# Block-sorted attention and a maxout MLP on one Trainium2 core: the hand-written order of the first batch item's steps is replaced by another

## The chip, the cores and the metric

The kernel runs on one core of a Trainium2 chip. The metric is the device time of one execution in microseconds, as the median of several runs. Lower is better. All times below are microseconds unless marked otherwise.

The engines are named as the profile names them: PE is TensorE's matmuls and PEld its weight loads, DVE is VectorE, ACT is ScalarE, POOL is GpSimd, SP is SyncE. POOL and SP mostly issue DMAs here.

## The reference

There are 4 batch items of 8 heads, 768 tokens and a head dimension of 64. Each head's tokens are cut into 8 blocks of 96. A small matrix per head is normalized five times by rows and columns, and mixes the key and value blocks. Each query block then attends to its own mixed block, and the result goes through an MLP with a maxout.

```python
P = sort_net                                  # (4, 8, 8, 8)
for _ in range(5):
    P = np.exp(P - np.max(P, axis=-1, keepdims=True))
    P = P / (np.sum(P, axis=-1, keepdims=True) + 1e-09)
    P = P / (np.sum(P, axis=-2, keepdims=True) + 1e-09)
k_sorted = np.einsum('bhij,bhjcd->bhicd', P, k_b)
v_sorted = np.einsum('bhij,bhjcd->bhicd', P, v_b)
scores = scale * np.matmul(q_b, k_sb.transpose(0, 1, 2, 4, 3))
attn = softmax(scores)                        # over the 96 keys of the block
x = np.matmul(attn, v_sb)                     # to (3072, 512)
...
out = np.maximum(x @ w1, x @ w2) @ w_out      # w1, w2: (512, 1024); w_out: (1024, 512)
```

## The kernel before

The kernel computes the maxout as `relu(x @ (w1 - w2)) @ w_out + x @ (w2 @ w_out)`. So `w1` is first replaced by the difference (`w_difference`, four quarters of the columns), and the product of `w2` and `w_out` is computed once (`w2_transposes`, then `w_product`).

The work of one item is cut into steps. Each step is a run of matmuls into one PSUM tile, followed by one eviction (or two instructions for the values) on VectorE or ScalarE. The steps that the change reorders are these, with the names that the order's text gives them:

- `k0` to `k2` (`sort_k`, line 449): mix a third of the keys' block positions with the sort matrix, 32 matmuls, eviction into `kT`.
- `v0` to `v3` (`sort_v`, line 473): the same for a quarter of the value dimensions, 16 matmuls, eviction into `v_sb`. Every one of them needs the whole of `v_dc`, which `turn_v` (line 242) makes from the raw values.
- `tq0`, `tq1` (`q_transposes`, line 413): transposes of two head pairs of the queries, 24 matmuls, eviction into `qT`.
- `SC0` to `SC7` (`scores`, line 539): 8 matmuls, then an exp on ScalarE into an `e` buffer. Scores 0, 1, 4, 5 read the first half of `qT`, and 2, 3, 6, 7 the second.
- `VA0` to `VA7` (`values`, line 567): 8 matmuls with `e` of the same number as weights, then a reciprocal (`rs`) and a product (`x`) on VectorE. It needs all of `v_sb`.
- `tx0` to `tx3` (`x_transposes`, line 600): transposes of two values' results, eviction into `xT`.
- `tw0`, `tw1` (`w2_transposes`, line 634): transposes of half of `w2`, eviction into `w2T`.
- `hcta`, `hctb` (`moe_h_products` and `moe_h`, lines 670 and 685): the two halves of the products of one hidden pair of tiles, 4 matmuls each. `c` is the half of the tokens, `t` the quarter of the hidden columns. The `a` half needs `tx0` (`c`=0) or `tx2` (`c`=1), the `b` half `tx1` or `tx3`. The relu eviction follows the `b` half.
- `diff2`, `diff3`: `w_difference` on VectorE. Differences 0 and 1 are done by POOL, ahead of this order.
- `pe2` (`block_diagonals`, line 312): the sort matrices for the later items, 5 matmuls and seven VectorE instructions.

A letter `A` or `D` at the end of a name fixes the eviction's engine, ScalarE or VectorE. `F` and a digit adds a 512-column matmul of zeros (`keep_streaming`, line 77) ahead of the matmuls of the next scores, values or first h half. The first key step has 640 such columns.

All engines take their own instructions in the order of the program (`manual_schedule`). All PSUM tiles come from one pool of four buffers (`psum`, tag `ps`), so a step's matmuls also wait until an earlier step's eviction has left a buffer. A pair of h halves holds its buffer from the `a` half to the eviction.

The order of the first item's steps is the text `front`. Between its last 26 steps and the ones before them, the POOL queue is given the loads of the next items' queries, values and keys. After `front`, the loops over the items run, with steps of the next item woven between products of the present one by the tables `first_tail`, `second_tail` and `third_tail`. They begin with the second item's keys (`KS`).

Of the kernel before, what the change touches and what calls it, by code (L numbers as in the profile page):

```python
# [16 lines left out]
def kernel(  # L17
# [752 lines left out]
    for b in range(1, B):  # L770
# [10 lines left out]
    turn_v(first, "D", 80, 96)  # L781

    front = """
        k0D k1A k2D v1D v2A v3A tq0D v0A tq1D SC1 SC0 F1
        SC2 VA1 SC5 VA0 SC3 F2 VA2 SC4 F0 tx0D SC6 VA3
        SC7 h00a VA4 tx1A tw0D h01a VA5 h01bA diff2 h00bA VA7 tx2A
        tw1A h02a VA6 h02bA h11a diff3 tx3A h12a h03a h12bD h10a h10bA
        pe2 h11bD h03bA h13a h13bA
    """.split()
    fills = [0]  # L790

# [170 lines left out]
```

The softmax here doesn't subtract the row's maximum and nothing guards it: scores larger than these inputs give would overflow.

## Time and profile before

| | |
|---|---|
| median of 4 runs | 166.57 us (166.44 to 167.0) |
| the profiled execution's own time | 166.44 us |
| its span | 164.7 us |
| PE busy | 159.1 us, 97% of the span |
| DVE busy | 76.3 us, 46% |
| ACT busy | 83.1 us, 50% |
| first key sort of item 0 starts | 11.94 us |
| first key sort of item 1 starts | 38.24 us |

The span runs from the first to the last instruction of the program on the core. The device time has 1.7 us more around it. Busy time of PE is an upper view, since its matmuls overlap. Times in the timeline and in the chain of waits count from the start of the span. The stretch between the two last rows of the table is the first item's front, in which the changed order stands.

### The profile page before, as it was taken

The numbers are of one execution on the slowest core, as the hardware profiler recorded it, in microseconds if no ns is written. First come the engines' busy times: TensorE is split into PE (matmuls) and PEld (weight loads), VectorE is DVE, ScalarE is ACT, GpSimd is POOL, SyncE is SP. The second block draws the span as 40 slices with busy tenths as digits, with TensorE's granted clock in tenths as the row PEclk, the third lists the DMA queues.
The fourth block names the chain that finished last, engine by engine and source line by source line (L and its number), as shares of the span: only waits on it lengthen the run. The fifth ranks groups of instructions, "written<-read, shape, count | busy, mean of one in ns | idle before, by whom it ended". The sixth has DMA issues, their size and how long they took to land.

```text
span 164.7 us, 4563 instructions
## 1 busy us (share of the span) xinstructions
PE 159.1 (97%) x2018; PEld 96.3 (58%) x2018; DVE 76.3 (46%) x169; ACT 83.1 (50%) x102; POOL 32.6 (20%) x59
## 2 busy tenths in 40 slices
PE   7999799999999999999999999999999999999992
PEld 7958578756554555557655554575655546654451
DVE  4879678556375564535277863250642320000011
ACT  3586895918239846055652262557447206642020
POOL 7999397140104000000014010000000000000000
DMA  3999999999999996688425999691025294000333
GB/s 48 204 205 197 199 208 205 210 203 221 212 202 211 219 236 100 175 116 218 90 27 100 192 189 234 166 226 23 0 52 175 50 164 142 0 0 0 127 131 127
DMA packets 30404, 23.90 MB, mean 145 GB/s; under 512 B 16752, under 2 KB 25200, under 8 KB 30384
## 3 DMA queue, kind: packets, MB, share of 16 engines
q0 software_dynamic: 11040, 13.37, 48.2%
q1 hardware_dynamic: 19200, 10.17, 26.9%
q8 instruction: 16, 0.26, 0.6%
q10 hardware_dynamic: 144, 0.07, 0.1%
q14 instruction: 4, 0.03, 0.1%
HBM read 26.75 MB, written 6.29 MB: 201 GB/s over the span
## 4 chain that ended last, share of the span: by engine, by line
PE 89%; DVE 5%; ACT 2%; issue 1%; DMA 1%
PE out_ps L704 38%; PE h_ps L677 26%; PE o_ps L575 5%; PE wc_ps L657 4%; PE k_ps L458 4%; PE s_ps L548 4%; PE tq_ps L433 2%; PE v_ps L479 1%; PE v_ps L523 1%; PE tw_ps L638 1%; ACT e L556 1%; DMA p_sb<-in_sort_net_dram 1%; PE tx_ps L613 1%; DVE colsum L276 1%; DVE p_sb L273 1%
## 5 line engine op out<-in xcount | busy, mean ns | idle before, releaser
L704 PE MATMUL out_ps<-wo_sb,g 128*128 128x512 bf16 (+2 forms) x200 | 48.3, 371 | 0.1
L677 PE MATMUL h_ps<-xT,w_sb 128*128 128x384 bf16 x256 | 44.5, 326 | 0.0
L677 PEld LDWEIGHTS <-w_sb 128*128 128x128 bf16 x256 | 24.0, 98 | 15.6
L556 ACT ACTIVATE e<-s_ps 96x768 bf16<-96x768 f32 x32 | 23.9, 804 | 13.9 <-PE s_ps L548 13.7
L691 ACT ACTIVATE g<-h_ps 128x768 bf16<-128x768 f32 x27 | 21.8, 811 | 17.4 <-PE h_ps L677 17.3
L704 PEld LDWEIGHTS <-g 128*128 128x128 bf16 x200 | 17.1, 97 | 15.8
L704 PE MATMUL out_ps<-wc,xT 128*128 128x512 bf16 (+2 forms) x100 | 24.8, 370 | 0.0
L108 ACT COPY o<-out_ps 128x1024 f32<-128x1024 f32 x10 | 10.1, 1012 | 28.0 <-PE out_ps L704 25.2
L592 DVE TENSOR_TENSOR x<-o_ps,rs 96x512 bf16<-96x512 f32 x32 | 22.0, 687 | 1.1
L704 PEld LDWEIGHTS <-xT 128*128 128x128 bf16 x100 | 9.6, 97 | 11.2
L575 PEld LDWEIGHTS <-e 96*128 96x128 bf16 x256 | 11.8, 97 | 5.9 <-DVE v_sb L110 0.2
L586 DVE RECIPROCAL rs<-o_ps 96x8 f32<-96x8 f32 x32 | 6.4, 201 | 18.0 <-PE o_ps L575 17.8
L739 DVE COPY o<-out_ps 128x512 f32<-128x512 f32 (+1 forms) x2 | 1.2, 624 | 27.6 <-PE out_ps L704 27.6
L575 PE MATMUL o_ps<-v_sb,e 96*128 96x65 bf16 x256 | 12.9, 193 | 0.0
L110 DVE CAST kT<-k_ps 128x1024 bf16<-128x1024 f32 x7 | 8.3, 1216 | 9.2 <-PE k_ps L458 9.2
L108 ACT CAST v_sb<-v_ps 96x1024 bf16<-96x1024 f32 x10 | 9.8, 1013 | 2.4 <-PE v_ps L479 0.9
L693 DVE TENSOR_SCALAR g<-h_ps 128x768 bf16<-128x768 f32 x5 | 4.8, 957 | 10.8 <-PE h_ps L677 10.8
L110 DVE CAST v_sb<-v_ps 96x1024 bf16<-96x1024 f32 x6 | 7.3, 1218 | 5.1 <-PE v_ps L523 2.2
L548 PE MATMUL s_ps<-qT,kT 64*128 64x96 bf16 x256 | 8.6, 204 | 1.0 <-PE o_ps L575 0.8
L160 POOL DMA_DIRECT2D v_raw<-in_k_dram x3 | 2.5, 833 | 35.2 <-DVE v_dc L250 31.4
L548 PEld LDWEIGHTS <-kT 64*128 64x128 bf16 x256 | 6.1, 94 | 5.8 <-issue 4.0
L169 POOL DMA_DIRECT2D v_raw<-in_v_dram x11 | 5.9, 540 | 13.7 <-DVE v_dc L250 8.3
(95 smaller groups left out, 144.5 us busy)
## 6 DMA issues: line engine op xcount, KB each, us to landing
out_dram<-o SPq DMA_DIRECT2D x11, 512.0 KB, 3.2
v_raw<-in_v_dram POOLq DMA_DIRECT2D x8, 384.0 KB, 12.5
k_raw<-in_k_dram POOLq DMA_DIRECT2D x9, 256.0 KB, 10.0
w_sb<-in_moe_w_dram POOLq DMA_DIRECT2D x4, 256.0 KB, 9.8
w_sb<-in_moe_w_dram POOLq DMA_DIRECT2D x2, 512.0 KB, 11.2
wo_sb<-in_moe_w_out_dram POOLq DMA_DIRECT2D x2, 512.0 KB, 14.6
v_raw<-in_v_dram POOLq DMA_DIRECT2D x3, 256.0 KB, 4.8
q_raw<-in_q_dram POOLq DMA_DIRECT2D x4, 192.0 KB, 9.0
```

The costliest lines, as they stand in the source:

```text
L108: nc.scalar.copy(out=out_ap, in_=in_ap)
L110: nc.vector.tensor_copy(out=out_ap, in_=in_ap)
L458: nc.tensor.matmul(ps[r0 : r0 + 64, m * 64 : (m + 1) * 64], kv[r0 : r0 + 64, t * 16 + m, :], bd_k[b][r0 : r0 + 64, :], start=True, stop=True,)
L548: nc.tensor.matmul(ps[:, h2 * 512 + ii * 128 : h2 * 512 + ii * 128 + BLK], kT[b][rows, (hp * 8 + i) * BLK : (hp * 8 + i) * BLK + 128], rhs ...
L556: nc.scalar.activation(out=e[:, 0 : 8 * BLK].rearrange("p (t c r) -> p t c r", t=8, r=R), in_=ps[0:BLK] .rearrange("p (t f) -> p t f", t=8 ...
L575: nc.tensor.matmul(ps[:, h2 * 512 + ii * 65 : h2 * 512 + (ii + 1) * 65], e[:, (h2 * 4 + ii) * BLK : (h2 * 4 + ii) * BLK + 128], v_sb[:, m0 ...
L586: nc.vector.reciprocal(out=rs, in_=ov[:, :, :, 64])
L592: nc.vector.tensor_tensor(out=x, in0=ov[:, :, :, 0:D], in1=rs.to_broadcast([BLK, 2, 4, D]), op=ALU.mult,)
L657: nc.tensor.matmul(ps[:, 0:512], w2T[:, fb, dmt * 128 : (dmt + 1) * 128], wo_sb[:, fb, :], start=(fb == 0), stop=(fb == NFB - 1),)
L677: nc.tensor.matmul(h_ps[ch, t][:, m * 512 : m * 512 + TCH], w1_sb[:, hp, fb * 128 : (fb + 1) * 128], xT[:, b % 2, ch, hp % 2, hp // 2, :], ...
L691: nc.scalar.activation(out=g, in_=src, func=AF.Relu)
L704: nc.tensor.matmul(dst, g_tiles[b, ch, m // 2][:, m % 2, off : off + 128] if m < NFB else xT[:, b % 2, ch, hp % 2, hp // 2, off : off + 12 ...
```

## The change

The text `front` is replaced. The same steps are in it, with these differences:

- The first key tile leaves PSUM by ScalarE, not VectorE. The value tiles come in the order 0, 3, 1, 2 with the first on VectorE, where they came as 1, 2, 3, 0.
- After the first two scores come one values step and one scores step, where it was scores first. There are four fills, not three.
- `SC6` and `SC5` stand next to each other; `SC7` comes only after `VA5`. `tw0` and `tx1` stand ahead of the first h products.
- `diff3` stands ahead of `VA5` and `diff2` after it.
- Seven steps follow `pe2`, where four did.
- Transposes 2 and 3 of x are evicted by VectorE instead of ScalarE, and of the eight h tiles VectorE takes three (`h03`, `h13`, `h10`), where it took two.

No function is changed.

```diff
     front = """
-        k0D k1A k2D v1D v2A v3A tq0D v0A tq1D SC1 SC0 F1
-        SC2 VA1 SC5 VA0 SC3 F2 VA2 SC4 F0 tx0D SC6 VA3
-        SC7 h00a VA4 tx1A tw0D h01a VA5 h01bA diff2 h00bA VA7 tx2A
-        tw1A h02a VA6 h02bA h11a diff3 tx3A h12a h03a h12bD h10a h10bA
-        pe2 h11bD h03bA h13a h13bA
+        k0A k1A k2D v0D v3A v1A tq0D v2A tq1D SC1 SC0 F3
+        VA1 SC3 F0 VA0 SC2 F2 VA3 SC4 F1 tx0D VA2 SC6
+        SC5 tw0D tx1A h00a h01a VA6 h00bA VA4 diff3 h01bA VA5 SC7
+        diff2 tw1A h03a VA7 h03bD h02a tx2D h02bA tx3D h13a pe2 h10a
+        h13bD h10bD h12a h11a h12bA h11bA
     """.split()
```

## The prediction

> **What bounds the kernel now.** I read the page first, then the chain of waits, then TensorE's timeline over the stretch that the change touches.
>
> ```profile
> span 164.7 us, 4563 instructions
> PE 159.1 (97%) x2018; PEld 96.3 (58%) x2018; DVE 76.3 (46%) x169; ACT 83.1 (50%) x102; POOL 32.6 (20%) x59
> q8 instruction: 16, 0.26, 0.6%
> PE 89%; DVE 5%; ACT 2%; issue 1%; DMA 1%
> ```
>
> TensorE is busy for 97% of the span and is 89% of the chain that ended last. The other engines matter only where TensorE stops for them. From the start of the item 1 keys (38.24) to the end the chain is nearly all matmuls, so what the front gains or loses should arrive at the end one for one. The question is where TensorE stops between the first key sort (11.94) and 38.24. The chain of waits over that stretch says:
>
> ```profile
> 16.95 0.81 PE tq_ps L433 x24
> 17.76 0.02 issue
> 17.78 0.97 DVE qT L110
> 18.75 0.04 issue
> 18.79 0.35 PE s_ps L548 x8
> 19.14 0.36 PE o_ps L575 x8
> 19.50 0.75 issue
> 20.25 0.34 PE s_ps L548 x8
> ```
>
> The columns are start, length and what the time went to. There are two stops. SC2 waits for the second query eviction (0.97 on VectorE). Then comes 0.75 of "issue", in which nothing in the profile releases TensorE. After 20.25 TensorE runs without a gap to 38.24. Its own timeline shows both:
>
> ```profile
> 18.79 0.35 PE L548 MATMUL s_ps<-qT,kT 64*128 64x96 bf16 x8 [0.28 <-DVE qT L110]
> 19.07 0.42 PE L575 MATMUL o_ps<-v_sb,e 96*128 96x65 bf16 x8
> 20.25 0.34 PE L548 MATMUL s_ps<-qT,kT 64*128 64x96 bf16 x8 [0.76 <-PE o_ps L575]
> 20.52 0.42 PE L575 MATMUL o_ps<-v_sb,e 96*128 96x65 bf16 x8
> ```
>
> The 0.76 stands at SC5. Its PSUM buffer (SC1's, read until 18.87), qT and kT were all ready, so a semaphore is not the reason. Queue q8 moved 16 packets of 16 KB. TensorE has 2018 + 2018 instructions, so q8 looks like its code. The packet records have one from 17.81 to 18.77 and the next at 23.84.
>
> **The change part by part.** The same 50 steps run; one fill matmul is added (four for three). The durations are this trace's, start to start: v sort 0.55, query transposes 0.79, scores 0.28 (0.18 before another scores), values 0.244 (0.35 before scores), x transposes 0.34, w2 transposes 0.93, half an h product 0.65, a fill 0.23 (0.31 before scores); ScalarE k/v eviction 1.01 (back to back every 0.91), exp 0.81 (0.70), VectorE k/v eviction 1.20 (1.13), values' rs and x 0.20 and 0.69. I let each engine take its queue in order with these numbers. As a test, the old order so worked, the 0.76 put in, reaches h00a at 23.55 (trace 23.56) and the end of the front at 38.06 (trace 38.24).
>
> *k0 to ScalarE, the v labels rotated.* In both orders three v tiles stand ahead of tq0, and one between tq0 and tq1.
>
> ```profile
> 12.98 2.34 DVE L110 CAST kT<-k_ps 128x1024 bf16<-128x1024 f32 x2
> 13.18 1.01 ACT L108 CAST kT<-k_ps 128x1024 bf16<-128x1024 f32 x1 [0.86 <-PE k_ps L458]
> ```
>
> k0 now leaves VectorE, which is busy with v_dc until 13.05, for ScalarE, idle until 13.18. Key evictions end at 14.98 for 15.33, ScalarE takes five for four, and v2, the last value tile, is out at 17.95 for 18.00. The Trainium skill (ScalarE: Activation LUTs, Rules for kernel authors) speaks against such a move: its table sends relu, max, add and mul to VectorE as faster per element, and read over to a copy, k0 would better stay there. The row decides otherwise for this fp32 copy out of PSUM, 1.01 against 1.20. Even if ScalarE were the slower by that 0.2, k0 would hide behind tq0 and tq1. By the row tq1 starts about 0.1 earlier (16.74 for 16.88; its last piece of q lands at 16.50). Either way VA1 waits for SC1's exp, so this part is worth 0 to -0.1.
>
> *The first scores.* Old: SC1 SC0 fill SC2 VA1 | SC5. New: SC1 17.53, SC0 17.71, fill 18.0, VA1 18.77 (SC1's exp ends 18.73), SC3 19.12 to 19.39. The wait for the query eviction becomes one for an exp of the same length. Behind VA1 on TensorE stands SC3, and ScalarE gets SC3's scores 0.08 after it is free. By 19.4 both orders have done three scores and one values. Gain 0.
>
> *The 0.76.* The trace cannot show if it returns, so it is bounded: 0 if it belonged to SC5, the full 0.86 (19.39 to 20.25) if it is code arriving. Row: TensorE's instruction records up to the stop number 705, and the new order gets to that number just after SC3, at 19.39. Rule: the Trainium skill (Runtime: NRT & Kernel Launch, Instruction fetch mechanics) has code coming in blocks of 16 KiB, 256 instructions, and the crossing of a boundary "mostly hidden". By the rule nothing stops there and the front ends at 37.35, 0.71 sooner. By the trace the page's block size fits q8 (4036 / 256 = 15.8 packets), but this boundary was not hidden: TensorE had used its last 256 instructions in 5.2 us (14.1 to 19.3), since sorts and transposes are short matmuls, while loads ran at the 200 GB/s of the page's row. Over the next 256 it took 7.7 us and did not stop. Both orders ask for the block at the same place, so I take the stop as staying, until 20.25. Both ends stay in the range.
>
> *From 20.25 on.* Left in both: five scores, seven values, four x and two w2 transposes, all h. The differences: one more fill (+0.23); values before scores four times for three (+0.11); SC6 and SC5 adjacent (-0.10); a fill ahead of values for one ahead of scores (-0.09). Sum +0.15. New starts: fill 20.25, VA0 20.47, SC2 20.82, VA3 21.32, tx0 21.94, VA2 22.51, SC6 22.86, SC5 23.04, tw0 23.32, tx1 24.25, h00a 24.59, h01a 25.24, VA4 26.78, tw1 28.30, h02a 30.78, tx2 31.43, h13a 32.76, pe2 33.41, end 38.21 (38.06 for the old, worked alike).
>
> *Waits that could grow.* h01a needs the POOL difference of w1, done at 24.29: 0.95 of slack. diff3 now stands ahead of VA5 on VectorE; it needs the w1 columns, landed 27.18, and comes up at 28.09, so VA5's rs and x behind it do not wait; h02a then needs diff2, done 30.23, slack 0.55. VectorE takes three g evictions for two and three xT for one, and ScalarE drops them: VectorE is solid from 26.7 to 37.4, and h13a and h13b have about 0.8 of slack on tx2 and tx3. pe2's bd is done by 35.6, before the keys need it. Edits at nothing thus hide behind the h products; without that cover the two xT copies alone would be 1.1.
>
> *Queues.* No step that moved issues a DMA. POOL's and SP's own orders stay. The split 26 steps from the end now falls after h00a and not VA4, but POOL reaches those loads at 25.86, and what they overwrite (q_raw, v_raw, k_raw) was read by 17.6. The q load into w2_sb is issued at 41.01, long after the last w2 reader in either order.
>
> **The sum.** 0 + 0 + 0.15 = +0.15 on the profiled execution: 166.44 (span 164.7 and 1.7 around it) becomes 166.6. That execution is the lowest of the four; their median is 166.57, so the median should be 166.7.
>
> **The rivals.**
> *The stop goes away* (the change does more than reorder). For: it stood exactly where SC5 begins, and the new order has no SC5 there. Against: nothing SC5 needed was late. Then -0.71: 165.9.
> *VectorE becomes the bound*, the slower side. Place: 28 to 34, where diff3, VA5, diff2, VA7, h03b, tx2, tx3 and the five bd masks queue in this order. For: no gap is left in its queue, and only one xT eviction has been seen on VectorE (0.54); at ScalarE's 0.80 the end is 0.33 later. Against: the same queue worked for the old order gave its first g eviction at 34.12 (trace 34.09). It decides once VectorE is over 0.6 to 0.8 late at tx2; later w1 columns do it too, from 1.2 after 27.18 and then one for one. Lateness of 1.4 to 1.6 costs 0.8: 167.5.
> *Another code stop, or a clock drop.* The next block ends in VA5 (27.9); the old order got to the same number at 27.92 unharmed. The granted clock is 1.00 in every stretch of before. Another stop of 0.76 makes 167.4.
>
> **How the numbers follow.** A change of 0.3% (0.5 us) is about what a measurement of this kernel can tell from none. The stop stays, forecast, 0.52: own range 166.3 to 167.2 (code 0.2 earlier to 0.5 of small waits); 0.40 same, 0.09 slower, 0.03 faster. The stop goes, 0.24: 0.20 faster, 0.04 same. VectorE late, 0.17: 0.15 slower, 0.02 same. Another stop, 0.07, slower. Faster 0.23, same 0.46, slower 0.31. The 80% range reaches to the first rival (165.8) and to the second (167.6).
>
> **What would show it.** Right: "issue" of 0.7 to 0.9 before the fill ahead of VA0, ended near 20.2; VA1 ended by the SC1 exp; no TensorE gap from there to the keys of item 1, which start at 38.3 to 38.5. Wrong, if VA0 starts at 19.6 and those keys at 37.6 (first rival); if h02a, h13a or h13b waits for VectorE (second); or if a gap stands at another step.

## The result, and the profile after

The changed kernel takes 167.09 us in the median (40 runs) beside 166.71 for the kernel before (61 runs of the same session). All ratios here leave out the runs that took over 1.5% longer than the fastest of the same kernel. The ratio is 1.0029, with a 95% interval of 1.0016 to 1.0043. That is 0.48 us slower (0.27 to 0.72), so it lies about at the bound that the prediction called measurable. A second test on another chip, told below, gave 0.9997 (0.9972 to 1.0022). Forecast were 166.7 and +0.15.

The page of the changed kernel, its lines for the span, the busy times, the code queue and the chain:

```profile
span 165.8 us, 4562 instructions
PE 159.1 (96%) x2019; PEld 95.9 (58%) x2019; DVE 77.3 (47%) x171; ACT 82.2 (50%) x100; POOL 32.8 (20%) x59
q8 instruction: 16, 0.26, 0.6%
PE 85%; DMA 5%; DVE 4%; ACT 2%; issue 2%
```

TensorE has just the one fill more, and two evictions went from ScalarE to VectorE on balance. The work is the same, yet the span grew by 1.13 in this execution. The last line says where to look: DMA was 1% of the chain and is now 5%.

First the chain of waits in the stretch where the prediction worked (start, length, what the time went to):

```profile
18.14 0.82 ACT e L556
18.95 0.05 issue
19.00 0.42 PE o_ps L575 x8
19.42 0.29 PE s_ps L548 x8
19.71 1.05 issue
20.77 0.39 PE o_ps L82
21.16 0.24 PE o_ps L575 x8
```

Here the forecast holds step by step. The first wait of TensorE is now VA1 (line 575), for an exp, where it was SC2, for a query eviction. SC3 follows. Then TensorE stops ahead of the new fill (line 82), at the same instruction record as before, 706, and with nothing that releases it. The stop was forecast at 0.86 until 20.25; in this execution it was 1.05 and ended at 20.77. From there TensorE has no gap until the keys of item 1, which begin at 38.84.

The part of the chain that was not forecast lies 40 us later:

```profile
71.62 2.25 PE h_ps L677 x14
73.87 6.26 DMA qT<-q_pair
80.13 0.14 issue
80.26 0.52 PE s_ps L548 x16
```

TensorE's own timeline of the changed kernel shows the price of it, in the bracket at the end of the line:

```profile
77.09 2.77 PE L677 MATMUL h_ps<-xT,w_sb 128*128 128x384 bf16 x16
80.26 0.52 PE L548 MATMUL s_ps<-qT,kT 64*128 64x96 bf16 x16 [0.40 <-DMA qT<-q_pair]
```

The first scores of item 2 wait 0.40 for their queries, which for items after the first are transposed by a DMA. Before, the same line stood without a bracket:

```profile
79.19 0.52 PE L548 MATMUL s_ps<-qT,kT 64*128 64x96 bf16 x16
```

So the 1.13 of these two executions is made of three parts (rounded): 0.52 from a stop that ended later, 0.08 from the stop's end to the keys of item 1 (18.08 for 18.00), and 0.52 from those keys to the end (126.94 for 126.42), of which 0.40 is the wait for the queries. The question for the runs is which of the three belong to the change.

### The profile page after: what moved, and what is told of

It reads as the page before. It is cut to its first block, busy times and chain, and to the rows that moved or that the text cites. A ratio compares the mean times of both kernels' runs of the same rounds, so it can differ in the third digit from the quotient of the medians.

```text
span 165.8 us, 4562 instructions
## 1 busy us (share of the span) xinstructions
PE 159.1 (96%) x2019; PEld 95.9 (58%) x2019; DVE 77.3 (47%) x171; ACT 82.2 (50%) x100; POOL 32.8 (20%) x59
## 4 chain that ended last, share of the span: by engine, by line
PE 85%; DMA 5%; DVE 4%; ACT 2%; issue 2%
PE out_ps L704 37%; PE h_ps L677 23%; PE o_ps L575 5%; PE wc_ps L657 4%; PE s_ps L548 4%; DMA qT<-q_pair 4%; PE k_ps L458 3%; PE tq_ps L433 2%; ACT e L556 2%; PE v_ps L479 1%; PE tw_ps L638 1%; PE v_ps L523 1%; DMA p_sb<-in_sort_net_dram 1%; PE tx_ps L613 1%; DVE colsum L276 1%
## 5 line engine op out<-in xcount | busy, mean ns | idle before, releaser
L691 ACT ACTIVATE g<-h_ps 128x768 bf16<-128x768 f32 x26 | 21.0, 811 | 19.6 <-PE h_ps L677 19.5
L110 DVE CAST kT<-k_ps 128x1024 bf16<-128x1024 f32 x6 | 7.2, 1222 | 10.7 <-PE k_ps L458 10.7
L693 DVE TENSOR_SCALAR g<-h_ps 128x768 bf16<-128x768 f32 x6 | 5.6, 953 | 9.2 <-PE h_ps L677 5.4
L82 PEld LDWEIGHTS <-fill 128*128 128x128 bf16 x92 | 7.3, 121 | 2.6 <-issue 1.2
```

What stands on the lines that cost most here:

```text
L82: nc.tensor.matmul(ps[:, 0:w], w0, fill[:, 0:w], start=True, stop=True)
L110: nc.vector.tensor_copy(out=out_ap, in_=in_ap)
L691: nc.scalar.activation(out=g, in_=src, func=AF.Relu)
```

## The experiments

All times of a stage come from one profiled execution of each kernel. This table holds what the text below uses. "Packet" is the start of one packet of 8 KB on queue q14, which the profile names an instruction queue (the third after the span's start), counted from the keys of item 1; starts and lengths of single packets are read from the trace's packet records; "qT" is the landing of item 2's first transposed queries, counted the same way.

| kernel | stop ended | keys of item 1 | keys less stop | packet | qT | wait for qT |
|---|---|---|---|---|---|---|
| before | 20.24 | 38.24 | 18.00 | 35.3 | 40.49 | 0 |
| old order again (e5) | 20.53 | 38.52 | 17.99 | 35.2 | 40.60 | 0 |
| after | 20.77 | 38.84 | 18.08 | 39.9 | 41.28 | 0.40 |
| new order again (e1) | 20.23 | 38.31 | 18.08 | 39.7 | 41.05 | 0.16 |
| old, fourth fill (e7) | 20.25 | 38.57 | 18.32 | 36.8 | 40.97 | 0.08 |
| new, x evictions on ScalarE (e9) | 20.25 | 38.38 | 18.13 | 25.4 | 40.63 | 0 |
| new, k0 on VectorE (e10) | 20.24 | 38.32 | 18.08 | 39.9 | 41.31 | 0.42 |
| new front half, old back half (e11) | 20.33 | 38.97 | 18.64 | 36.9 | 40.70 | 0 |
| old front half, new back half (e12) | 20.23 | 38.50 | 18.26 | 40.8 | 42.21 | 1.33 |

**The two orders once more (e1, e5).** No edit; they tell what one execution of the same program does differently from another.

> The new order unchanged, for a second profile and an interval. Theory (the stop is TensorE's code arriving late): the stop stands again at TensorE's record 706, ahead of the fill of VA0, ends between 20.2 and 20.8, and the ratio to the old order is 1.001 to 1.004. Rival (something in the step SC5, or chance): no stop, or at another record. If the wait of 0.4 for the transposed queries near 80 us belongs to the change it is there again; if it is chance it is gone.

> The old order unchanged, for a second profile. Theory: a stop at record 706 (SC5) again, ended 5.7 to 6.2 after record 449; the length differs by some tenths from execution to execution, as the start of the code packet does. If this length is the spread of the runs, the stop ends between 20.2 and 20.8 as in the new order's two profiles.

e1: ratio 0.9997 (0.9972 to 1.0022). e5: 0.9995 (0.9968 to 1.0021). The stop ended at 20.23 in e1, where it had been 20.77. In the old order it ended at 20.53, where it had been 20.24. TensorE's timeline of e5:

```profile
20.53 0.34 PE L548 MATMUL s_ps<-qT,kT 64*128 64x96 bf16 x8 [1.02 <-issue]
```

So the stop varies by 0.5 from execution to execution in both orders, and the 0.52 between the profiles of before and after is no effect of the change. What stays the same in both pairs is the column "keys less stop": 18.00 and 17.99 for the old order, 18.08 twice for the new one. It is also one more look at the wait for the queries: 0.16 in the new order, none in the old.

**Is the stop late code? (e3, e4).** Both orders with 26 TensorE records fewer ahead of the first item. The warm-up's columns of zeros are cut into fewer, longer matmuls. If the stop hangs on a block of 256 records, it moves to another step. (A record is one TensorE instruction in the trace, a matmul or a weight load.)

```diff
-    keep_streaming(ps_f32("fill_ps"), 86 * 126, most=126)
+    keep_streaming(ps_f32("fill_ps"), 86 * 126, most=150)
```

> The old order; the 86 warm-up matmuls of 126 columns are 73 of 150, the same streaming time with 26 fewer TensorE records, so that every later step stands 26 records earlier. Theory (code blocks of 256): record 705 now lies inside VA0/SC3, the request is also 26 records later in the work; the stop leaves SC5, shrinks to 0.2 to 0.5 inside VA0 or SC3, and the time falls by 0.2 to 0.5. Rival (the stop belongs to SC5): 0.76 stays ahead of SC5 and the time stays. Rival (chance DMA): stop anywhere, time the same on the median.

> The same for the new order. Theory: record 706 now lies inside SC2; the stop ahead of VA0 goes, one of 0.2 to 0.5 stands inside SC2, and it is 0.4 to 0.6 faster than the new order, so about 0 to 0.2 faster than the old order unchanged and 0.1 to 0.2 slower than the old order with 26 fewer records. Rival (the stop belongs to the step): it stays ahead of VA0 and the time stays.

e3 took 170.86, ratio 1.025 (1.0222 to 1.0278). e4 took 171.42, ratio 1.0305 (1.0274 to 1.0335). The stop left SC5 and VA0. It now stood in a value sort, at record 450, which is 706 less 256, and it was much longer. TensorE's timeline of e3:

```profile
17.37 0.67 PE L479 MATMUL v_ps<-bd,v_dc 64*128 64x64 bf16 x17 [2.58 <-issue]
```

In e4 the stop was 2.76, ended at 17.39, at the same record. No step of the program is special there: the counted records are. The size was a surprise. The request for a block is in no trace. By the count of 256, the block that is needed at 450 should be asked for one block earlier, at about record 193. With 26 records fewer, that record comes to lie behind TensorE's wait for the sort matrix instead of ahead of it, at 11.5 for 10.2, and the first 16 KB packet on q8 starts at 15.04 (14.94 in e4) instead of 11.75. With the stop the granted clock went to 0.5 for 6.8 us in both, and the rest of the 4 to 5 us lies in that stretch.

**What makes the block late? (e8).** The old order, but all weight loads, the two differences on GpSimd and item 1's keys wait until the second query eviction has left PSUM. This alters when the data moves, not what TensorE does until 19.5. The kernel pays for it later with a wait of 4.88 for the weights, so only the stretch to 20 is of interest.

```diff
+        if step == "tq1D":
+            held = const.tile([128, 32], BF16, tag="held", name="held")
+            nc.gpsimd.tensor_copy(out=held, in_=qT[0][:, 2, 0, 0:32])
+            for t in range(2):
+                load_w_columns(w2_sb, moe_w2, t, t + 1)
...
+            load_k(1)
```

> The old order, with the loads of the MLP's weights and what POOL does after them put behind a POOL copy that waits for the second query eviction (near 18.8). h steps then wait for weights, so the time is some 10 us longer and says nothing; asked is the stop at record 706. Theory (the code's packet waits behind the weights' traffic): between record 449 and the packet's start lie less than 3.5 us, no stop or one under 0.3 at record 706. Rival (the request itself takes this long, whatever else moves): the packet starts 3.5 after record 449 as before and the stop of 0.7 to 0.9 stays.

The stretches of 2 us before and in e8, one after the other. The columns are the stretch, its length, the busy time (and the instructions) of PE, PEld, DVE, ACT and POOL, TensorE's granted clock, the busy share of the DMA engines, and what the DMA queues moved, in GB/s:

```profile
14.00:16.00 2.00, 1.94 (x59) 1.67 (x57) 2.00 (x3) 1.29 (x3) 1.97 (x5) 1.00 1.38 197
16.00:18.00 2.00, 2.00 (x70) 1.76 (x64) 1.60 (x3) 1.83 (x2) 1.32 (x2) 1.00 1.47 203
```

```profile
14.00:16.00 2.00, 1.94 (x58) 1.67 (x55) 2.00 (x3) 1.29 (x3) 0.00 (x0) 1.00 0.68 104
16.00:18.00 2.00, 2.00 (x70) 1.77 (x66) 1.60 (x3) 1.84 (x2) 0.00 (x0) 1.00 0.05 12
```

And TensorE's timeline of e8 at the place where the stop had stood:

```profile
19.15 0.42 PE L575 MATMUL o_ps<-v_sb,e 96*128 96x65 bf16 x8
19.50 0.34 PE L548 MATMUL s_ps<-qT,kT 64*128 64x96 bf16 x8
19.77 0.42 PE L575 MATMUL o_ps<-v_sb,e 96*128 96x65 bf16 x8
```

SC5 starts at 19.50 without a bracket: the stop is gone. Record 449, where by the same count the block for record 706 should be asked for, is reached at 14.35 (before 14.27). The second packet of code starts at 16.01 in e8, 1.66 after it, and at 17.81 before, 3.54 after it. So the packet came 1.9 sooner when the weights were not moving. That is the cause of the stop, as far as this one execution shows it: TensorE used 256 records of sorts and transposes in 5 us, and the block it needed next came behind 200 GB/s of weights.

**The fills (e2, e6, e7).** The new order with one fill taken out in two places, and the old order with a fourth one.

```diff
-        VA1 SC3 F0 VA0 SC2 F2 VA3 SC4 F1 tx0D VA2 SC6
+        VA1 SC3 VA0 SC2 F2 VA3 SC4 F1 tx0D VA2 SC6
```

> The new order without the fill ahead of VA0. Theory: one fill of 0.23 less after the stop, which now ends inside VA0, two records later; 0.2 faster than the new order unchanged, so 0 to 0.3 slower than the old order. Rival (a fill is free because the stop covers it): no difference to the new order. Rival (fills keep the clock up): the granted clock falls below 1.00 and it is over 1 us slower.

```diff
-        VA1 SC3 F0 VA0 SC2 F2 VA3 SC4 F1 tx0D VA2 SC6
+        VA1 SC3 F0 VA0 SC2 F2 VA3 SC4 tx0D VA2 SC6
```

> The new order without the fill ahead of VA2; the one at the stop stays. Theory of the sum (a fill after the stop costs its 0.23): 0.2 faster than the new order, ratio to the old order 0.999 to 1.002. Rival (tx0 or an eviction ends last there, so that a fill is free): as the new order. Rival (every fill is needed for the clock): over 0.5 slower, with a granted clock below 1.00.

```diff
-        SC2 VA1 SC5 VA0 SC3 F2 VA2 SC4 F0 tx0D SC6 VA3
+        SC2 VA1 F3 SC5 VA0 SC3 F2 VA2 SC4 F0 tx0D SC6 VA3
```

> The old order with a fourth fill, ahead of SC5, where TensorE stops. Theory: the fill comes after the code and costs 0.31 (before scores): item 1's keys start 0.3 later, the time is 0.3 above the old order and equals the new order's within 0.2. Rival (the difference of the two orders lies in the later half, VectorE's evictions): the keys start 0.3 later here too, but the new order's stay apart from this by another 0.2 or more.

e2 (without the fill ahead of VA0): 1.0044 (1.0019 to 1.0068). e6 (without the one ahead of VA2): 1.0007 (0.9986 to 1.0028). e7: 0.9993 (0.9974 to 1.0012). In the trace of e7 the fourth fill, ahead of scores, makes "keys less stop" 18.32, 0.32 more than the old order's and the 0.31 that the prediction has for such a fill. The runs do not show those 0.32: their interval ends at +0.2. And no fill that was taken out made the new order measurably faster. The profiled executions of e2 and e6 cannot be compared by stage: in both the granted clock fell right after the stop, for 3.4 us from 21.02 in e2 and for 6.8 us from 21.34 in e6. A stretch of e2 (the clock is the third number from the end):

```profile
21.00:24.50 3.50, 3.50 (x52) 2.50 (x50) 2.48 (x6) 1.61 (x2) 2.39 (x2) 0.51 1.25 210
```

Their stops were 0.80 and 0.96 long, no longer than those of after (1.05) and e5 (1.02), which left the clock at 1.00. So the stop can cost more than its length, and its length alone does not decide it. That a fill costs its 0.32 ahead of scores is shown in the trace of e7, but not by the times, and what hides it is open.

**The first key tile (e10).**

```diff
-        k0A k1A k2D v0D v3A v1A tq0D v2A tq1D SC1 SC0 F3
+        k0D k1A k2D v0D v3A v1A tq0D v2A tq1D SC1 SC0 F3
```

> The new order with the first key tile's eviction back on VectorE. My prediction puts that part at 0 to 0.1 to the good, so this costs 0 to 0.1: the values step after the first two scores still waits for the exp, and item 1's keys start at 38.3 to 38.4 for a stop that ends at 20.23. The rival, that the key tile's engine frees the buffers or the queries' evictions earlier than I worked out: the first scores start 0.2 to 0.4 later, and item 1's keys as much later, unless the stop at record 706 swallows it. Ratio to the old order 0.998 to 1.003.

VA1 is again ended by the exp, after a gap of 0.41, the stop ended at 20.24, and item 1's keys start at 38.32, with 38.31 in e1. The first key tile does gain something ahead of the stop: counted from item 0's first key sort, the second query transposes start after 4.79 in after and e1 and after 4.94 before and in e10. The stop swallows these 0.15, so this part is worth 0. The ratio, 1.0048 (1.003 to 1.0065), is 0.80 us; the profile, with its wait of 0.42, accounts for 0.63 of it.

**Whose is the wait for the queries? (e9, e11, e12).** e9 is the new order with two evictions on another engine, e11 and e12 are the two halves of the change.

```diff
-        diff2 tw1A h03a VA7 h03bD h02a tx2D h02bA tx3D h13a pe2 h10a
+        diff2 tw1A h03a VA7 h03bD h02a tx2A h02bA tx3A h13a pe2 h10a
```

> The new order with the evictions of x transposes 2 and 3 back on ScalarE, so that ScalarE has 102 instructions and VectorE 169 as in the old order. The theory that the instruction counts decide when the 8 KB instruction packet near 80 us comes: it returns to about 35.3 us after item 1's keys, and the wait of item 2's first scores for the transposed queries (0.16 to 1.0 in the new order) is gone, so that keys to end is 126.4 to 126.5 and not 126.7 to 126.9. The theory that the wait is an accident of the execution, or follows from the keys' start alone: the packet stays near 40 after the keys and a wait of 0.1 to 1.0 stays. On the front: my prediction had h13a some 0.8 ahead of a late VectorE; with ScalarE doing the two copies item 1's keys should start within 0.15 of the new order's at an equal stop (38.3 for a stop that ends at 20.23). Ratio to the old order 0.997 to 1.002 by the first theory.

e11, as a difference to the new order:

```diff
-        SC5 tw0D tx1A h00a h01a VA6 h00bA VA4 diff3 h01bA VA5 SC7
-        diff2 tw1A h03a VA7 h03bD h02a tx2D h02bA tx3D h13a pe2 h10a
-        h13bD h10bD h12a h11a h12bA h11bA
+        SC5
+        SC7 h00a VA4 tx1A tw0D h01a VA5 h01bA diff2 h00bA VA7 tx2A
+        tw1A h02a VA6 h02bA h11a diff3 tx3A h12a h03a h12bD h10a h10bA
+        pe2 h11bD h03bA h13a h13bA
```

> The new order up to the sixth scores, then the old order from SC7 on. It separates the two halves of the change. If the wait of item 2's first scores for the transposed queries belongs to the back half (its evictions on VectorE), it is gone and keys to end is 126.4 to 126.5. If it belongs to the front half, it stays at 0.1 to 1.0. Item 1's keys: the front half has one more fill (0.23 by my sum), so about 0.1 to 0.2 later than the old order's at an equal stop. Ratio to the old order 1.000 to 1.002 in the first case, 1.001 to 1.005 in the second.

e12, as a difference to the old order:

```diff
-        SC7 h00a VA4 tx1A tw0D h01a VA5 h01bA diff2 h00bA VA7 tx2A
-        tw1A h02a VA6 h02bA h11a diff3 tx3A h12a h03a h12bD h10a h10bA
-        pe2 h11bD h03bA h13a h13bA
+        tw0D tx1A h00a h01a VA6 h00bA VA4 diff3 h01bA VA5 SC7
+        diff2 tw1A h03a VA7 h03bD h02a tx2D h02bA tx3D h13a pe2 h10a
+        h13bD h10bD h12a h11a h12bA h11bA
```

> The old order up to VA3, then the new order from w2's first transposes on (differences 3 and 2 interchanged, three relu evictions and two of x on VectorE). If the back half's counts on ScalarE and VectorE bring the wait of item 2's first scores, it shows here: 0.1 to 1.0, with the 8 KB packet near 40 after item 1's keys. If not, no wait. Item 1's keys within 0.15 of the old order's at an equal stop (38.24 for a stop that ends at 20.24) if VectorE keeps up, 0.3 or more later if VectorE is late at the x transposes.

Ratios: e9 1.0021 (0.9999 to 1.0043), e11 1.0058 (1.0032 to 1.0085), e12 1.0066 (1.005 to 1.0083), which is 1.10 us. The profiled execution of e12 took 168.14, above the median of 167.54, so its wait is longer than the usual one. Two lines of TensorE's timelines, e9 and then e12, at the first scores of item 2:

```profile
79.34 0.51 PE L548 MATMUL s_ps<-qT,kT 64*128 64x96 bf16 x16
```

```profile
80.85 0.52 PE L548 MATMUL s_ps<-qT,kT 64*128 64x96 bf16 x16 [1.33 <-DMA qT<-q_pair]
```

In these profiles the wait belongs to the back half: it is in e12 and not in e11. Within the back half it belongs to the engine of two copies of x at 32 us: e9 differs from the new order in nothing else, and there the wait is gone. The times agree: e9 and e10 ran in the same test, with medians of 166.83 and 167.44, and apart from the first key tile they differ in these two copies alone. The old back half has neither.

Stretches of half a microsecond show how the transposes lose the time. First the changed kernel, where the 8 KB packet runs from 78.72 to 79.13; then e9, which has none near there; then e12, packet from 79.31 to 79.72:

```profile
78.70:79.20 0.50, 0.50 (x5) 0.29 (x3) 0.00 (x0) 0.50 (x1) 0.00 (x0) 1.00 1.41 270
79.20:79.70 0.50, 0.50 (x5) 0.20 (x2) 0.00 (x0) 0.21 (x1) 0.00 (x0) 1.00 1.70 36
79.70:80.20 0.50, 0.16 (x1) 0.00 (x0) 0.00 (x0) 0.30 (x1) 0.00 (x0) 1.00 0.96 217
```

```profile
77.80:78.30 0.50, 0.50 (x5) 0.31 (x4) 0.28 (x1) 0.16 (x1) 0.00 (x0) 1.00 1.28 284
78.30:78.80 0.50, 0.50 (x5) 0.31 (x4) 0.00 (x0) 0.50 (x1) 0.00 (x0) 1.00 1.32 244
78.80:79.30 0.50, 0.50 (x4) 0.15 (x2) 0.00 (x0) 0.15 (x1) 0.00 (x0) 1.00 1.22 272
```

```profile
79.30:79.80 0.50, 0.21 (x2) 0.00 (x0) 0.00 (x0) 0.25 (x1) 0.00 (x0) 1.00 1.87 277
79.80:80.30 0.50, 0.00 (x0) 0.00 (x0) 0.00 (x0) 0.50 (x1) 0.00 (x0) 1.00 0.87 25
80.30:80.80 0.50, 0.00 (x0) 0.00 (x0) 0.00 (x0) 0.06 (x1) 0.00 (x0) 1.00 0.98 221
```

The transposes run at about 280 GB/s. Directly after the packet they fall to 25 or 36 for half a microsecond, and then go on. This is so in all seven profiles with the new back half and the two copies on VectorE (after, e1, e2, e4, e6, e10, e12). In the other seven profiles the packet comes 2.8 us earlier or more, and the transposes run through that place without a pause, in e7 and e11 at only about 190 to 250 GB/s. What sets the packet's time is open. It repeats between executions of one kernel (35.3 and 35.2, 39.9 and 39.7) and it moved with the two copies, but in e9 it came at 25.4 and not back at 35.3, and in e7 a fill on TensorE alone moved it to 36.8.

That the packet itself makes the pause is what the order in time suggests; no run moved this packet alone. The packets of 16 KB on q8 say the same. In twelve of the fourteen profiles one of them starts 34.2 to 35.4 after item 1's keys, and the transposes of x that were issued at 33.06 land at 37.4 to 37.7. In e3 and e4, where 26 records are gone, that packet comes at 38.3; the same transposes land at 35.8 to 35.9, and the pause is behind the moved packet, in the transposes of the queries. In e3, packet from 80.72 to 81.93:

```profile
80.80:81.30 0.50, 0.50 (x4) 0.30 (x4) 0.50 (x2) 0.50 (x1) 0.00 (x0) 1.00 2.05 185
81.30:81.80 0.50, 0.50 (x5) 0.29 (x3) 0.50 (x1) 0.01 (x1) 0.00 (x0) 1.00 2.44 27
81.80:82.30 0.50, 0.50 (x5) 0.29 (x3) 0.35 (x1) 0.04 (x1) 0.00 (x0) 1.00 0.07 7
```

This pause comes with a wait of 0.24 in the old order. Instruction packets are not the whole of it either. In e12 the transposes also stood nearly still from 77.1 to 78.4, with no such packet, and this is why its wait is the longest; e2 has a pause of that kind too, from about 38.5 after item 1's keys, and e8 a shorter one. These are unexplained.

e11 shows one thing more, which was not expected. Its "keys less stop" is 18.64:

```profile
24.22 0.81 PE L677 MATMUL h_ps<-xT,w_sb 128*128 128x384 bf16 x4 [0.58 <-DVE x L592]
```

SC6, SC5 and SC7 then stand in a row, each with a PSUM buffer, so the first h product waits for a buffer that VectorE's product of the values (line 592) has not left. In the new order SC7 comes only after VA5, and this wait does not occur. The new halves fit each other.

## Why the prediction was right, and where it was not

The median of 167.09 lies within the predicted range, 0.4 from the predicted 166.7, and the small loss had the right sign. But only part of it is the loss that was worked out: +0.15 lies below the interval of the first test (0.27 to 0.72) and within that of the second, and most of what the traces show beyond it comes from a place where the prediction put nothing. That the number came so near is in part luck.

- *k0 to ScalarE, 0 to -0.1*: right. The second query transposes came 0.15 sooner after the first key sort, where about 0.1 was forecast. e10 undoes it and moves item 1's keys by 0.01.
- *The first scores, gain 0*: right. The wait for a query eviction (0.28) became one for an exp (0.41). VA1 came at 19.00 for 18.77, but in that execution item 0's first key sort began at 12.17 and not at 11.94; counted from it, VA1 stands at 6.83, as worked out. What the first scores gain or lose is swallowed by the stop behind them.
- *The stop stays*: right, at the same record and for the reason given. The first rival, that it goes and 165.9 results, fell with the first profile. e3 and e4 show that the record decides and e8 that the traffic does. Of the rule that was weighed against the row (the Trainium skill, Runtime: NRT & Kernel Launch, Instruction fetch mechanics), the blocks of 256 instructions agree with the stops at 450 and 706. "Mostly hidden" does not, at these places: 0.5 to 1.1 us in the profiles of the two orders and 2.6 to 2.8 in e3 and e4. Wrong was to treat its end, 20.25, as a constant. It is 20.23 to 20.77 in the executions of the two orders, and it follows the code packet, which starts at 17.8 before and in e1, and at 18.3 in after and e5.
- *From 20.25 on, +0.15*: the measured number at an equal stop is +0.08. The terms are right in kind; the mis-sized part is the first stretch after the stop. h00a starts at 24.51 in e1, 0.08 sooner than the 24.59 worked out: 0.02 because the stop ended at 20.23, 0.03 because w2's transposes took 0.90 instead of 0.93, and 0.03 from the other steps together. From h00a on, both orders ran 0.17 to 0.18 longer than worked out, which cancels.
- *VectorE becomes the bound*: it did not. The x copies ran from 32.47 and 33.40, and no h product waited for them. e9 takes them off VectorE, and "keys less stop" is 18.13 for 18.08.
- *The step that failed* is in the first part: "what the front gains or loses should arrive at the end one for one". It did not look at the stretch behind the keys for anything that the front could shift there, and so has no case for the wait of item 2's first scores. That wait is 0.16 and 0.40 in the two profiles of the new order, and 0.42 in e10; with it the stretch behind the keys grew by 0.26 and 0.52 in the former two, where the prediction has 0. In the old order those queries landed 0.35 to 0.46 before their use (40.49 and 40.60 for 40.95), which the trace of before did show; the prediction checked slack at 24 to 37 us and not there.

The sum as it stands: +0.08 in the front and +0.26 to +0.52 behind the keys make 0.34 to 0.60, against +0.48 (0.27 to 0.72) by the first test and -0.05 (-0.47 to +0.37) by the second. e9, which keeps the new order and loses only the wait, would be left with +0.13 to 0.16 by the trace; its runs give +0.35 (-0.02 to +0.72). No version was measurably faster than the kernel before, and both orders lose 0.5 to 1.1 to a stop that neither of them sets, and more where the clock falls after it.

## What to carry to other kernels

A stop on an engine with no releaser, at the same instruction count in two orders of the same work, was code that came late here. Moving the data traffic removed it (e8); reordering did not. Compare orders from the end of such a stop, since its length varies more than the change is worth. And when a reorder moves work from one engine to another, look through the whole trace for waits with little slack, also far behind the edit: here two copies at 32 us brought a wait at 80 us.

## What the runs showed of the hardware

A change of 26 records in the warm-up, with the same columns streamed, cost 4 to 5 us (2.5% and 3.05%). By the count of records, it moved a request for code behind TensorE's wait for the sort matrix. The granted clock went to 0.5 for 6.8 us with the stop of 2.6 to 2.8. Stops of 0.5 to 1.1 us in before, after, e1 and e5 left it at 1.00, but after stops of 0.80 in e2 and 0.96 in e6 it went to 0.5 for 3.4 and 6.8 us.

Code packets on q8 stood behind data: 3.5 to 4.0 us from record 449 to the packet's start under about 200 GB/s of loads (before, after, e1, e5), and 1.66 when the loads had nearly stopped (e8). The packet itself took 0.9 to 1.0 us in either case, and after a stop TensorE went on 1.3 to 1.5 us after its end.

An 8 KB instruction packet was followed by a pause of about half a microsecond in a DMA transpose, in all seven profiles in which it came while item 2's queries were being transposed. A 16 KB packet went with a longer one: where it was shifted by 3 us (e3, e4), a transpose that it had met before landed 1.6 to 1.8 us sooner.
